# Four stages of a TensorE-bound kernel written in another order: FFT stages placed among matmul blocks, scaled grad_out kept on chip, w2 loaded early

## The chip, the cores and the metric

One core of a Trainium2 chip. The time is device microseconds (us) from start to end of one execution. A profile's *span* is the time from the first to the last instruction of one profiled execution, about 1.8 us below the time of that same execution.

## The reference

A gated sum of two branches and all its gradients:

```python
g = sigmoid((x * gate_w).sum(-1))             # x: [2048, 1024]
a = irfft2(rfft2(x) * (w_r + 1j * w_i))       # spectral branch
h = relu(B_x @ w1 + b1) ** 2                  # w1: [1024, 3584]
b = h @ w2 + b2                               # w2: [3584, 1024]
out = g * a + (1 - g) * b
# returned: out and the gradients of x, w_r, w_i, w1, b1, w2, b2, gate_w
```

The gradients of the dense branch flow only to its weights and, through the gate, to x. Work per stage, as the kernel cuts it:

- **rows, first FFT stage**: x and grad_out are transposed in blocks, the gate is computed, and each of 16 row tiles of x and of grad_out goes through the first transform (32 steps).
- **spectra**: 8 pairs of frequencies; forward transform, product with w, gradient of w, transform back (40 steps in the written program).
- **last FFT stage**: 32 steps, 16 for the output and 16 for the gradient of x.
- **h/dh**: 28 blocks of 128 hidden units, h and its gradient dh, with their transposes.
- **dW2, dW1**: 56 + 56 blocks of 16 matmuls.
- **out, input gradient**: 32 + 32 blocks of 28 matmuls.

## The kernel before

The kernel is written with a scheduler that orders each engine's instructions before the run. Tiles of one `tag` share `bufs` buffers. The parts that matter (cut):

```python
fps, fps_s = pool("fps", "right", PSUM)      # tag "ps2": 2 buffers of 2 banks, FFT stages
tps, tps_s = pool("tps", "right", PSUM)      # tag "tr": 2 buffers of 1 bank, transposes AND the spectra's small sp/si
...
# load_rows: for each of 16 row tiles
turned(xT, xt, i, nc.scalar.copy)            # 8 transposes, one copy
... gate of the row ...
db = fb.tile([P, D], BF16, name="db", tag="db", bufs=2)
nc.vector.tensor_scalar(out=db[:], in0=go[:], scalar1=omg[:, c_], ...)   # (1-g) * grad_out
turned(dbT, db, i, nc.vector.tensor_copy)    # only the transposed copy survives
one_s1(fb, cf, 0, i, xt, kf[:])              # first FFT stage of x
one_s1(fb, cf, 1, i, go, kg[:])              # ... and of grad_out
...
# mlp_grads: grad_out is loaded and scaled again, 16 times
ld(out=db[:], in_=go_perm[t])
nc.vector.tensor_scalar(out=db[:], in0=db[:], scalar1=omg[:, t : t + 1], ...)
...
# mlp_out: w2 (7 MB) is loaded at its start, w1T (7 MB) at its second block
for fc in range(0, FC, 4):
    ld(out=w2[:, fc : fc + 4, :], ...)
for k in range(S // BW):
    ...
    if k == 1:
        for fc in range(0, FC, 4):
            ld(out=w1T[:, fc : fc + 4, :], ...)
...
run(chain(load_rows(), fft_mid(), fft_out()))   # the order in which it is written
run(mlp_in())
run(mlp_grads())
...
run(mlp_out())
```

Of the kernel before, what the change touches and what calls it, by code (L numbers as in the profile page):

```python
# [10 lines left out]
P = 128  # L11
# [119 lines left out]
def kernel(  # L131
# [208 lines left out]
    def fft_mid():  # L340
# [3 lines left out]
        for m in range(S2 // 2):  # L344
# [5 lines left out]
            for T in range(2):  # L350
                z = fb.tile([P, 2, D], FDT, name="z", tag="z", bufs=3)
                ld(out=z[:], in_=z_scr[T][:].rearrange("c p l -> p c l")[:, m : m + 9 : 8, :])
                xs.append(spectrum(fb, T, m, z, am, sgn))
                yield 8
# [31 lines left out]
    def fft_out():  # L386
        fb, fbs = pool("f3", "right")
# [4 lines left out]
        for T in range(2):  # L392
            for i in range(NT):
# [20 lines left out]
                st(out=ax_scr[T][i][:], in_=yo[:])  # L414
                yield 2
        fbs.close()


    xT_p, xT_s = pool("xT")
# [3 lines left out]
    def load_rows():  # L423
        fb, fbs = pool("f1", "right")
        cf = fb.tile(list(consts["cf"].shape), FDT, name="cf", tag="cf")
        ld(out=cf[:], in_=cten["cf"].ap())
        b1row = fb.tile([FC, P], BF16, name="b1row", tag="b1row")
        ld(out=b1row[:], in_=B_b1.rearrange("(fc p) -> fc p", p=P))
        b1ps = tps.tile([P, FC], BF16, name="b1ps", tag="tr", bufs=2)
        nc.tensor.transpose(b1ps[:], b1row[:], identb[:FC, :FC])  # L430
        nc.vector.tensor_copy(out=b1col[:], in_=b1ps[:])
# [6 lines left out]

        for i in range(NT):
            xt = fb.tile([P, D], BF16, name="xt", tag="xt", bufs=3)  # L440
            ld(out=xt[:], in_=x_perm[i])
            turned(xT, xt, i, nc.scalar.copy)
            go = fb.tile([P, D], BF16, name="go", tag="go", bufs=3)
            ld(out=go[:], in_=go_perm[i])
            junk = fb.tile([P, D], BF16, name="junkt", tag="junkt")
            c_ = slice(i, i + 1)
            nc.vector.tensor_tensor_reduce(
                out=junk[:], in0=xt[:], in1=gatew_bc[:], scale=1.0, scalar=0.0,
                op0=ALU.mult, op1=ALU.add, accum_out=sgate[:, c_],
            )  # L450
            nc.scalar.activation(gcol[:, c_], sgate[:, c_], ACT.Sigmoid)
            nc.vector.tensor_scalar(out=omg[:, c_], in0=gcol[:, c_], scalar1=-1.0, scalar2=1.0, op0=ALU.mult, op1=ALU.add)
            db = fb.tile([P, D], BF16, name="db", tag="db", bufs=2)
            nc.vector.tensor_scalar(out=db[:], in0=go[:], scalar1=omg[:, c_], scalar2=None, op0=ALU.mult)
            turned(dbT, db, i, nc.vector.tensor_copy)
            kg = fb.tile([P, P], FDT, name="kg", tag="kg", bufs=2)
            nc.vector.tensor_scalar(out=kg[:], in0=kf[:], scalar1=gcol[:, c_], scalar2=None, op0=ALU.mult)
            one_s1(fb, cf, 0, i, xt, kf[:])
            one_s1(fb, cf, 1, i, go, kg[:])
            yield 8  # L460
        V(out=gpg[:], in0=gcol[:], in1=omg[:], op=ALU.mult)
# [77 lines left out]
    def column_sums(sb_pool, ps_pool, tag, acc, dst):  # L539

        row = sb_pool.tile([1, D], BF16, name="row", tag="row")
        for hf in range(NH):
            cs = slice(hf * H, (hf + 1) * H)
            pr = ps_pool.tile([1, H], FP32, name="prow", tag=tag, bufs=2)
# [5 lines left out]
    def mlp_grads():  # L550
        wb, wbs = pool("m2")
        mps, mpss = pool("mps2", "left", PSUM)
        res = []
        acc = wb.tile([P, D], FP32, name="dbacc", tag="dbacc")

        def group(scr, fg):
            t_ = wb.tile([P, NT, FGW], BF16, name="grp", tag="grp", bufs=2)
            ld(out=t_[:], in_=scr[fg][:])
            return t_

        nxt = None
        for t in range(NT):
            db = wb.tile([P, D], BF16, name=f"res0_{t}", tag=f"res0_{t}")
            ld(out=db[:], in_=go_perm[t])
            if t == 0:
                nxt = group(h2_scr, 0)
            nc.vector.tensor_scalar(out=db[:], in0=db[:], scalar1=omg[:, t : t + 1], scalar2=None, op0=ALU.mult)  # L567
            if t == 0:
                nc.vector.tensor_copy(out=acc[:], in_=db[:])
            else:  # L570
                V(out=acc[:], in0=acc[:], in1=db[:], op=ALU.add)
            res.append(db)
        jobs = [(h2_scr, fg) for fg in range(FG)] + [(dh_scr, fg) for fg in range(FG)]
        for n, (scr, fg) in enumerate(jobs):
# [10 lines left out]
            if scr is h2_scr:  # L585
                for fb_ in range(FGC):
                    wo = wb.tile([P, D], BF16, name="wo2", tag="wo2", bufs=2)
                    for hf in range(NH):
                        pw = mps.tile([P, H], FP32, name="pw", tag="pw", bufs=2)
                        for t in range(NT):  # L590
                            mm(  # L591
                                pw[:], lhsT=cur[:, t, fb_ * P : (fb_ + 1) * P], rhs=res[t][:, hf * H : (hf + 1) * H],
# [19 lines left out]
        wbs.close()  # L612

# [3 lines left out]
    def blocks(wb, scr):  # L617
        v_ = scr[:].rearrange("c p s -> p c s")

        def one(k):  # L620
            t_ = wb.tile([P, FC, BW], BF16, name="hblk", tag="hblk", bufs=2)
            ld(out=t_[:], in_=v_[:, :, k * BW : (k + 1) * BW])
            return t_
# [3 lines left out]
    def mlp_out():  # L627
        wp, wps = pool("w2p")
        w2 = wp.tile([P, FC, D], BF16, name="w2", tag="w2")
# [6 lines left out]
        for fc in range(0, FC, 4):  # L636
            ld(out=w2[:, fc : fc + 4, :], in_=B_w2[fc * P : (fc + 4) * P, :].rearrange("(q p) e -> p q e", p=P))
# [69 lines left out]
        column_sums(wb, mps, "acc2", gacc, out_8)  # L707
# [4 lines left out]
    def chain(*gens):  # L712
        for g_ in gens:
            yield from g_

    def run(gen):
        for _ in gen:
            pass

    run(chain(load_rows(), fft_mid(), fft_out()))  # L720
    run(mlp_in())
    run(mlp_grads())
    tps_s.close()
    fps_s.close()
    run(mlp_out())


# [28 lines left out]
```

## Time and profile before

| | kernel before |
|---|---|
| time, median of 3 | 1671.34 us (1670.29 to 1671.43) |
| span of the profiled run | 1667.4 us |
| mean granted TensorE clock | 0.948 |
| TensorE busy, VectorE busy | 1488.8 us (89%), 670.8 us (40%) |
| loads and stores | 267 MB, 160 GB/s |

TensorE is busy 89% of the span, but that counts slow matmuls and overlapping rows as full work. The slices and the stretches that the prediction prints are the better view: two regimes, one after the other, each with the other engine at rest.

### The profile page before, as it was taken

To read this page: it belongs to the slowest core of one execution; us is meant where nothing else is said; L and a number is where in the kernel's file an instruction comes from. 1 tells how busy PE (TensorE), PEld (TensorE's weight loads), DVE (VectorE), ACT (ScalarE), POOL (GpSimd) and SP (SyncE) were. 2 spreads that over 40 slices of the span, in tenths; PEclk is the share of its full clock that TensorE was granted. 3 is DMA by queue.
4 is the path that set the end of the run, shared out by engine and by line. 5 is a ranking of instruction groups with operands and counts; after the bars stand their busy time and mean duration, and the time that the engine had idled before them with its cause. 6 is when DMAs were issued, how large, how long until landed. Compare 5 with 4: busy or idle time off the path is not lost.

```text
span 1667.4 us, 20915 instructions
## 1 busy us (share of the span) xinstructions
PE 1488.8 (89%) x8482; PEld 732.5 (44%) x8482; DVE 670.8 (40%) x1334; ACT 437.2 (26%) x566; POOL 225.2 (14%) x395
## 2 busy tenths in 40 slices
PE   5655555799999999999959999999998999999997
PEld 4531111366555555555514444444443444444443
DVE  7846998666433333333361000000001555564232
ACT  6862222377533333333301111111110000000000
POOL 3330110122211111111110000111110000000000
PEclk9997676799999999999969999999999999999999
DMA  7536554468545655465488232323227853574340
GB/s 212 159 113 186 151 155 116 120 209 278 190 154 167 196 168 165 155 200 165 151 319 261 92 136 94 136 96 135 96 82 273 256 162 111 161 200 137 101 139 19
DMA packets 157194, 267.45 MB, mean 160 GB/s; under 512 B 10652, under 2 KB 90538, under 8 KB 155306
## 3 DMA queue, kind: packets, MB, share of 16 engines
q1 hardware_dynamic: 122890, 147.59, 28.6%
q0 software_dynamic: 34208, 118.53, 21.4%
q8 instruction: 66, 1.08, 0.3%
q14 instruction: 30, 0.25, 0.1%
HBM read 147.57 MB, written 118.51 MB: 160 GB/s over the span
## 4 chain that ended last, share of the span: by engine, by line
issue 68%; POOL 9%; PE 0%; ACT 0%; POOLq 0%; DVE 0%
POOL out_dram L609 2%; POOL dh_scr L524 1%; POOL out_dram L598 1%; POOL w1T_scr L510 1%; POOL h2T_scr L520 1%; POOL dhT_scr L521 1%; POOL ax_scr L414 1%; POOL out_dram L706 1%; POOL h_scr L523 1%; POOL out_dram L672 1%; PE pui L255 0%; ACT rt L401 0%; ACT e L405 0%; POOL out_dram L534 0%; POOLq L609 0%
## 5 line engine op out<-in xcount | busy, mean ns | idle before, releaser
L493 PE MATMUL ph<-xT,w1g 128*128 128x512 bf16 x896 | 226.8, 380 | 0.0
L591 PE MATMUL pw<-res,grp 128*128 128x512 bf16 x896 | 203.9, 388 | 18.0 <-DVE res L567 10.8
L499 PE MATMUL pd<-dbT,w2T 128*128 128x512 bf16 x896 | 215.3, 381 | 3.1 <-DVE w2T L486 3.1
L665 PE MATMUL acc<-w,hblk 128*128 128x512 bf16 x896 | 195.6, 382 | 6.1 <-DMA w<-in_B_w_dram 6.1
L666 DVE SCALAR_TENSOR_TENSOR ot<-acc,omg,af 128x512 bf16<-128x512 f32 x32 | 24.0, 750 | 437.7 <-PE acc L665 437.6
L603 PE MATMUL pw<-grp,res 128*128 128x512 bf16 x896 | 193.5, 379 | 0.0
L703 PE MATMUL accg<-w1Tr,hblk 128*128 128x512 bf16 x896 | 193.5, 379 | 0.0
L500 DVE SCALAR_TENSOR_TENSOR dhT<-pd,rT 128x512 bf16<-128x512 f32 x112 | 77.4, 691 | 258.2 <-PE pd L499 258.2
L591 PEld LDWEIGHTS <-grp 128*128 128x128 bf16 x896 | 88.7, 99 | 133.3 <-issue 26.4
L495 ACT ACTIVATE rT<-ph,b1col 128x512 bf16<-128x512 f32 x112 | 77.2, 689 | 238.6 <-PE ph L493 238.6
L665 PEld LDWEIGHTS <-hblk 128*128 128x128 bf16 x896 | 88.1, 98 | 113.6 <-DMA w<-in_B_w_dram 6.6
L499 PEld LDWEIGHTS <-w2T 128*128 128x128 bf16 x896 | 87.4, 98 | 106.5 <-DVE w2T L486 8.1
L703 PEld LDWEIGHTS <-hblk 128*128 128x128 bf16 x896 | 87.7, 98 | 105.7
L603 PEld LDWEIGHTS <-res 128*128 128x128 bf16 x896 | 87.7, 98 | 105.7
L493 PEld LDWEIGHTS <-w1g 128*128 128x128 bf16 x896 | 83.1, 98 | 72.7 <-issue 1.6
L595 ACT CAST wo<-pw 128x512 bf16<-128x512 f32 x56 | 32.7, 586 | 195.1 <-PE pw L591 195.1
L608 ACT CAST wo<-pw 128x512 bf16<-128x512 f32 x56 | 32.8, 586 | 160.6 <-PE pw L603 160.6
L255 PE MATMUL pu<-cf,ft 128*128 128x256 f16 (+3 forms) x256 | 38.7, 293 | 38.1 <-ACT ft L235 37.0
L496 ACT ACTIVATE h2T<-rT 128x512 bf16<-128x512 bf16 x112 | 70.6, 630 | 3.5
L704 DVE TENSOR_TENSOR gxo<-accg,g 128x512 bf16<-128x512 f32 x32 | 22.1, 691 | 105.1 <-PE accg L703 104.9
L319 PE MATMUL pv<-y,apmat 128*128 128x512 f16 x32 | 16.0, 549 | 53.9 <-DVE y L366 53.2
L609 POOL DMA_DIRECT2D out_dram<-wo x56 | 30.2, 540 | 163.2 <-ACT wo L608 158.7
(178 smaller groups left out, 1668.9 us busy)
## 6 DMA issues: line engine op xcount, KB each, us to landing
h2T_scr<-h2T POOLq DMA_DIRECT2D x28, 512.0 KB, 3.4
dhT_scr<-dhT POOLq DMA_DIRECT2D x28, 512.0 KB, 4.3
h_scr<-h2S POOLq DMA_DIRECT2D x14, 1024.0 KB, 8.0
dh_scr<-dhS POOLq DMA_DIRECT2D x14, 1024.0 KB, 10.6
grp<-h_scr SPq DMA_DIRECT2D x7, 2048.0 KB, 8.6
hblk<-h2T_scr SPq DMA_DIRECT2D x8, 1792.0 KB, 9.2
grp<-dh_scr SPq DMA_DIRECT2D x7, 2048.0 KB, 8.4
hblk<-dhT_scr SPq DMA_DIRECT2D x8, 1792.0 KB, 9.1
```

Of the source, the lines that this page charges most:

```text
L255: mm(pu[:, bank, lo : lo + n], lhsT=ft[:, b, :], rhs=mat[:, o : o + n], start=bool(f_ & 1), stop=bool(f_ & 2), skip_group_check=True,)
L493: mm(ph[:], lhsT=w1g[:, dc, fs], rhs=xT[:, dc, ss], start=(dc == 0), stop=(dc == DC - 1))
L495: nc.scalar.activation(rT[:], ph[:], ACT.Relu, bias=b1col[:, fc : fc + 1])
L496: nc.scalar.activation(h2T[:, ss], rT[:], ACT.Square)
L499: mm(pd[:], lhsT=w2T[:, ec, :], rhs=dbT[:, ec, ss], start=(ec == 0), stop=(ec == DC - 1))
L500: STT(out=dhT[:, ss], in0=pd[:], scalar=2.0, in1=rT[:], op0=ALU.mult, op1=ALU.mult, accum_out=gb1part[:, fc, sb : sb + 1],)
L591: mm(pw[:], lhsT=cur[:, t, fb_ * P : (fb_ + 1) * P], rhs=res[t][:, hf * H : (hf + 1) * H], start=(t == 0), stop=(t == NT - 1),)
L603: mm(pw[:], lhsT=xr[t][:, d_ * P : (d_ + 1) * P], rhs=cur[:, t, :], start=(t == 0), stop=(t == NT - 1),)
L608: nc.scalar.copy(out=wo[:], in_=pw[:])
L609: st(out=out_4[d_ * P : (d_ + 1) * P, fg * FGW : (fg + 1) * FGW], in_=wo[:])
L665: mm(acc[:], lhsT=cur[:, fc, t2 * P : (t2 + 1) * P], rhs=w2[:, fc, cs], start=(fc == 0), stop=(fc == FC - 1))
L703: mm(acc[:], lhsT=cur[:, fc, t2 * P : (t2 + 1) * P], rhs=w1T[:, fc, cs], start=(fc == 0), stop=(fc == FC - 1))
```

## The change

Its intent: put each piece of work that needs VectorE or ScalarE beside matmuls that don't. The core of the diff, cut:

```diff
+    dbn = db_p.tile([P, NT, D], BF16, name="dbn", tag="dbn")      # scaled grad_out, natural order, stays on chip
...
+        for i0 in range(0, NT, 4):          # four rows, then their x transforms, then one h/dh block
+            ...
+                nc.vector.tensor_scalar(out=dbn[:, i, :], in0=go[:], scalar1=omg[:, c_], ...)
+                turned(dbT, dbn[:, i, :], i, nc.vector.tensor_copy)
+            ...
+                one_s1(fb, cf, 0, i, xts[i - i0], kf[:])
+            yield
         for i in range(NT):                 # the grad_out transforms, later
             ...
+            one_s1(fb, cf, 1, i, go, kg[:])
+            yield
...
-            ld(out=db[:], in_=go_perm[t])   # mlp_grads: no second load and scaling
...
-                                pw[:], lhsT=cur[...], rhs=res[t][:, hf * H : (hf + 1) * H],
+                                pw[:], lhsT=cur[...], rhs=dbn[:, t, hf * H : (hf + 1) * H],
...
+                if T == 0 and i % 2 == 1:   # last FFT stage: w2 in pieces, long before out
+                    ...
+                        ld(out=w2[:, fc : fc + 4, :], ...)
...
-    run(chain(load_rows(), fft_mid(), fft_out()))
-    run(mlp_in())
-    run(mlp_grads())
+    for _ in rows:
+        for _ in range(1 if n < 4 else 6):  # h/dh units per row group, then per grad_out transform
+            next(units, None)
+    ...
+    for k, _ in enumerate(grads):           # spectra and half of the last stage among dW2/dW1
+        while done < todo * (k + 1) // per:
+            next(spec)
+            done += 1
+    for _ in outs:                          # the rest of the last stage among out
+        next(spec, None)
```

The spectra's z tile also goes from three buffers to two.

More of the change, by code (lines that the diff above doesn't have):

```diff
@@ L350, in fft_mid @@
             for T in range(2):
-                z = fb.tile([P, 2, D], FDT, name="z", tag="z", bufs=3)
+                z = fb.tile([P, 2, D], FDT, name="z", tag="z", bufs=2)
                 ld(out=z[:], in_=z_scr[T][:].rearrange("c p l -> p c l")[:, m : m + 9 : 8, :])
@@ L386, in fft_out @@
     def fft_out():
+        w2_p, w2_s = pool("w2p", "right")
+        w2 = w2_p.tile([P, FC, D], BF16, name="w2", tag="w2")
+        later["w2"], later["w2_s"] = w2, w2_s
         fb, fbs = pool("f3", "right")
@@ L414, in fft_out @@
                 st(out=ax_scr[T][i][:], in_=yo[:])
+                if T == 0 and i % 2 == 1:
+                    fc = 2 * (i - 1)
+                    if fc < FC:
+                        ld(out=w2[:, fc : fc + 4, :], in_=B_w2[fc * P : (fc + 4) * P, :].rearrange("(q p) e -> p q e", p=P))
                 yield 2
         fbs.close()
+    db_p, db_s = pool("db")
+    dbn = db_p.tile([P, NT, D], BF16, name="dbn", tag="dbn")
     xT_p, xT_s = pool("xT")
@@ L421, with rows_and_first_stage @@
     dbT = xT_p.tile([P, DC, S], BF16, name="dbT", tag="dbT")
-    def load_rows():
+    def rows_and_first_stage():
         fb, fbs = pool("f1", "right")
         cf = fb.tile(list(consts["cf"].shape), FDT, name="cf", tag="cf")
-        ld(out=cf[:], in_=cten["cf"].ap())
         b1row = fb.tile([FC, P], BF16, name="b1row", tag="b1row")
-        ld(out=b1row[:], in_=B_b1.rearrange("(fc p) -> fc p", p=P))
-        b1ps = tps.tile([P, FC], BF16, name="b1ps", tag="tr", bufs=2)
-        nc.tensor.transpose(b1ps[:], b1row[:], identb[:FC, :FC])
-        nc.vector.tensor_copy(out=b1col[:], in_=b1ps[:])
         def turned(dst, xt, i, eng):
@@ L437, in turned @@
             eng(out=dst[:, :, i * P : (i + 1) * P], in_=pt[:])
+        for i0 in range(0, NT, 4):
+            xts = []
+            for i in range(i0, i0 + 4):
+                xt = fb.tile([P, D], BF16, name="xt", tag="xt", bufs=4)
+                ld(out=xt[:], in_=x_perm[i])
+                xts.append(xt)
+            if i0 == 0:
+                ld(out=b1row[:], in_=B_b1.rearrange("(fc p) -> fc p", p=P))
+                b1ps = tps.tile([P, FC], BF16, name="b1ps", tag="tr", bufs=2)
+                nc.tensor.transpose(b1ps[:], b1row[:], identb[:FC, :FC])
+                nc.vector.tensor_copy(out=b1col[:], in_=b1ps[:])
+            for i in range(i0, i0 + 4):
+                xt = xts[i - i0]
+                c_ = slice(i, i + 1)
+                turned(xT, xt, i, nc.scalar.copy)
+                junk = fb.tile([P, D], BF16, name="junkt", tag="junkt")
+                nc.vector.tensor_tensor_reduce(
+                    out=junk[:], in0=xt[:], in1=gatew_bc[:], scale=1.0, scalar=0.0,
+                    op0=ALU.mult, op1=ALU.add, accum_out=sgate[:, c_],
+                )
+                nc.scalar.activation(gcol[:, c_], sgate[:, c_], ACT.Sigmoid)
+                nc.vector.tensor_scalar(out=omg[:, c_], in0=gcol[:, c_], scalar1=-1.0, scalar2=1.0, op0=ALU.mult, op1=ALU.add)
+                go = fb.tile([P, D], BF16, name="go", tag="go", bufs=3)
+                ld(out=go[:], in_=go_perm[i])
+                nc.vector.tensor_scalar(out=dbn[:, i, :], in0=go[:], scalar1=omg[:, c_], scalar2=None, op0=ALU.mult)
+                turned(dbT, dbn[:, i, :], i, nc.vector.tensor_copy)
+            if i0 == 0:
+                ld(out=cf[:], in_=cten["cf"].ap())
+            for i in range(i0, i0 + 4):
+                one_s1(fb, cf, 0, i, xts[i - i0], kf[:])
+            yield
@@ L439, in load_rows @@
+        V(out=gpg[:], in0=gcol[:], in1=omg[:], op=ALU.mult)
         for i in range(NT):
-            xt = fb.tile([P, D], BF16, name="xt", tag="xt", bufs=3)
-            ld(out=xt[:], in_=x_perm[i])
-            turned(xT, xt, i, nc.scalar.copy)
             go = fb.tile([P, D], BF16, name="go", tag="go", bufs=3)
             ld(out=go[:], in_=go_perm[i])
-            junk = fb.tile([P, D], BF16, name="junkt", tag="junkt")
-            c_ = slice(i, i + 1)
-            nc.vector.tensor_tensor_reduce(
-                out=junk[:], in0=xt[:], in1=gatew_bc[:], scale=1.0, scalar=0.0,
-                op0=ALU.mult, op1=ALU.add, accum_out=sgate[:, c_],
-            )
@@ L451, in load_rows @@
-            nc.scalar.activation(gcol[:, c_], sgate[:, c_], ACT.Sigmoid)
-            nc.vector.tensor_scalar(out=omg[:, c_], in0=gcol[:, c_], scalar1=-1.0, scalar2=1.0, op0=ALU.mult, op1=ALU.add)
-            db = fb.tile([P, D], BF16, name="db", tag="db", bufs=2)
-            nc.vector.tensor_scalar(out=db[:], in0=go[:], scalar1=omg[:, c_], scalar2=None, op0=ALU.mult)
-            turned(dbT, db, i, nc.vector.tensor_copy)
             kg = fb.tile([P, P], FDT, name="kg", tag="kg", bufs=2)
-            nc.vector.tensor_scalar(out=kg[:], in0=kf[:], scalar1=gcol[:, c_], scalar2=None, op0=ALU.mult)
@@ L458, in load_rows @@
-            one_s1(fb, cf, 0, i, xt, kf[:])
+            nc.vector.tensor_scalar(out=kg[:], in0=kf[:], scalar1=gcol[:, i : i + 1], scalar2=None, op0=ALU.mult)
             one_s1(fb, cf, 1, i, go, kg[:])
-            yield 8
-        V(out=gpg[:], in0=gcol[:], in1=omg[:], op=ALU.mult)
+            yield
         fbs.close()
@@ L537, in mlp_in, with column_sums @@
         xT_s.close()
-    def column_sums(sb_pool, ps_pool, tag, acc, dst):
+    def column_sums(sb_pool, ps_pool, tag, acc, dst, bufs=2):
         row = sb_pool.tile([1, D], BF16, name="row", tag="row")
@@ L543, in column_sums @@
             cs = slice(hf * H, (hf + 1) * H)
-            pr = ps_pool.tile([1, H], FP32, name="prow", tag=tag, bufs=2)
+            pr = ps_pool.tile([1, H], FP32, name="prow", tag=tag, bufs=bufs)
             mm(pr[:], lhsT=ones_f[:, 0:1], rhs=acc[:, cs], start=True, stop=True)
@@ L552, in mlp_grads @@
         mps, mpss = pool("mps2", "left", PSUM)
-        res = []
+        strm = later["strm"]
         acc = wb.tile([P, D], FP32, name="dbacc", tag="dbacc")
         def group(scr, fg):
-            t_ = wb.tile([P, NT, FGW], BF16, name="grp", tag="grp", bufs=2)
+            t_ = strm.tile([P, NT, FGW], BF16, name="grp", tag="strm", bufs=2)
             ld(out=t_[:], in_=scr[fg][:])
             return t_
-        nxt = None
-        for t in range(NT):
-            db = wb.tile([P, D], BF16, name=f"res0_{t}", tag=f"res0_{t}")
-            ld(out=db[:], in_=go_perm[t])
-            if t == 0:
-                nxt = group(h2_scr, 0)
-            nc.vector.tensor_scalar(out=db[:], in0=db[:], scalar1=omg[:, t : t + 1], scalar2=None, op0=ALU.mult)
-            if t == 0:
-                nc.vector.tensor_copy(out=acc[:], in_=db[:])
-            else:
-                V(out=acc[:], in0=acc[:], in1=db[:], op=ALU.add)
-            res.append(db)
         jobs = [(h2_scr, fg) for fg in range(FG)] + [(dh_scr, fg) for fg in range(FG)]
+        nxt = group(*jobs[0])
+        nc.vector.tensor_copy(out=acc[:], in_=dbn[:, 0, :])
+        for t in range(1, NT):
+            V(out=acc[:], in0=acc[:], in1=dbn[:, t, :], op=ALU.add)
         for n, (scr, fg) in enumerate(jobs):
@@ L591, in mlp_grads @@
                             mm(
-                                pw[:], lhsT=cur[:, t, fb_ * P : (fb_ + 1) * P], rhs=res[t][:, hf * H : (hf + 1) * H],
+                                pw[:], lhsT=cur[:, t, fb_ * P : (fb_ + 1) * P], rhs=dbn[:, t, hf * H : (hf + 1) * H],
                                 start=(t == 0), stop=(t == NT - 1),
@@ L612, in mlp_grads @@
         wbs.close()
+        db_s.close()
     BW = 2 * P
@@ L620, in one @@
         def one(k):
-            t_ = wb.tile([P, FC, BW], BF16, name="hblk", tag="hblk", bufs=2)
+            t_ = later["strm"].tile([P, FC, BW], BF16, name="hblk", tag="strm", bufs=2)
             ld(out=t_[:], in_=v_[:, :, k * BW : (k + 1) * BW])
@@ L627, in mlp_out @@
     def mlp_out():
-        wp, wps = pool("w2p")
-        w2 = wp.tile([P, FC, D], BF16, name="w2", tag="w2")
+        w2 = later["w2"]
+        wp, wps = pool("w1p")
         w1T = wp.tile([P, FC, D], BF16, name="w1Tr", tag="w1Tr")
@@ L635, in mlp_out @@
         nxt = load(0)
-        for fc in range(0, FC, 4):
-            ld(out=w2[:, fc : fc + 4, :], in_=B_w2[fc * P : (fc + 4) * P, :].rearrange("(q p) e -> p q e", p=P))
         for k in range(S // BW):
@@ L706, in mlp_out @@
                 st(out=o1_perm[t], in_=ot[:])
-        column_sums(wb, mps, "acc2", gacc, out_8)
+        column_sums(wb, mps, "acc", gacc, out_8, 4)
         mpss.close()
@@ L710, in mlp_out, with spectra @@
         wps.close()
-    def chain(*gens):
-        for g_ in gens:
-            yield from g_
-    def run(gen):
-        for _ in gen:
-            pass
-    run(chain(load_rows(), fft_mid(), fft_out()))
-    run(mlp_in())
-    run(mlp_grads())
-    tps_s.close()
+    later = {}
+    rows, units = rows_and_first_stage(), mlp_in()
+    n = 0
+    for _ in rows:
+        for _ in range(1 if n < 4 else 6):
+            next(units, None)
+        n += 1
+    strm_p, strm_s = pool("strm", "right")
+    later["strm"] = strm_p
+    for _ in units:
+        pass
+    def spectra():
+        yield from fft_mid()
+        yield from fft_out()
+    spec, grads = spectra(), mlp_grads()
+    todo = 5 * (S2 // 2) + NT
+    per = 2 * FG * FGC * NH
+    done = 0
+    for k, _ in enumerate(grads):
+        while done < todo * (k + 1) // per:
+            next(spec)
+            done += 1
+    tps_s.close()
+    outs = mlp_out()
+    for _ in outs:
+        next(spec, None)
+    for _ in spec:
+        pass
     fps_s.close()
-    run(mlp_out())
+    later["w2_s"].close()
+    strm_s.close()
 _INS = ['A_x', 'A_w_r', 'A_w_i', 'B_x', 'B_w1', 'B_b1', 'B_w2', 'B_b2', 'gate_w', 'grad_out']
```

## The prediction

> **What bounds the kernel now.** I read the page's slices first, then the costliest groups, then busy time by stretches that I cut at the stage borders, then the waits of TensorE, then timelines. The slices give the shape:
>
> ```profile
> PE   5655555799999999999959999999998999999997
> DVE  7846998666433333333361000000001555564232
> PEclk9997676799999999999969999999999999999999
> ```
>
> Each slice is 41.7 us. TensorE is at half in slices 0 to 7, full afterwards, with two dents: slice 20 (5, with the clock at 6) and slice 30. VectorE is near full in slices 2 to 7 and at 0 to 3 from slice 21 to 29. So the first 310 us are bound by other engines while TensorE idles, and the rest by TensorE while the others idle. Busy time by stretch (columns: stretch, its length, busy us of PE, PEld, DVE, ACT, POOL, the clock, the DMA share, GB/s):
>
> ```profile
> 8.70:125.00 116.30, 73.22 (x776) 56.91 (x776) 84.55 (x225) 87.31 (x98) 41.37 (x95) 1.00 0.50 159
> 125.00:310.00 185.00, 99.40 (x461) 35.12 (x461) 157.50 (x244) 45.44 (x39) 20.40 (x29) 0.69 0.52 143
> 310.00:445.00 135.00, 128.59 (x1004) 78.11 (x1004) 81.30 (x229) 88.25 (x102) 31.51 (x53) 0.95 0.67 217
> 445.00:843.00 398.00, 397.33 (x2650) 209.53 (x2647) 141.39 (x308) 149.43 (x214) 63.86 (x95) 1.00 0.53 168
> 843.00:878.00 35.00, 17.06 (x35) 4.41 (x36) 25.99 (x36) 1.07 (x2) 3.30 (x3) 0.53 1.02 388
> 878.00:1261.60 383.60, 382.25 (x1763) 172.28 (x1761) 5.30 (x7) 63.87 (x109) 45.35 (x84) 1.00 0.34 121
> 1261.60:1463.00 201.40, 195.34 (x896) 88.15 (x897) 100.78 (x200) 0.59 (x1) 8.63 (x16) 0.98 0.63 199
> ```
>
> The first row is the first FFT stage with the rows' transposes, the second the spectra (VectorE busy 157.5 of 185 us), the third the last FFT stage, already mixed with the h/dh blocks. So the order in which the program is written is not quite the order in which it runs: instructions of later stages were moved up where nothing held them. Then come h/dh alone, a gap, dW2 and dW1, and out; after 1463 us the same for the input gradient.
>
> ```profile
> PE pv L319 <- DVE y L366: 53.2, 16, 5.2
> PE pu L255 <- ACT ft L235: 37.0, 30, 1.9
> PE px L292 <- DVE pm L281: 22.5, 8, 3.0
> PE pw L591 <- DVE res L567: 10.8, 15, 1.6
> PE acc L665 <- DMA w<-in_B_w_dram: 6.1, 1, 6.1
> ```
>
> These are TensorE's waits (us in all, times, longest): on the spectra's VectorE products, on ScalarE's copy between the two matmuls of the first stage, on grad_out being scaled a second time, and on w2 being loaded at the start of out. Each is a thing that the change goes at.
>
> **What the Trainium skill says.** Four places bear on this.
> - "TensorE: Matmul & The Clock Gate", section "What's actually happening": the array runs at half clock by default and reaches full clock only after a sustained busy window. The trace agrees: clock 0.69 in the spectra and 0.53 in the gap at 843 us, 1.00 elsewhere. So gaps cost twice, once as idle time and once as slow matmuls after them.
> - The same page, "Step-by-step: what each phase is for": weight loads may be pulled ahead, but matmuls stay in program order. A spectrum matmul placed too early among the dW2 blocks therefore holds up the blocks behind it. The trace before can't show that for the spectra; for the last FFT stage it shows how little it can cost (below).
> - "Perfetto Trace Analysis", "Optimization Strategy": where the most-contended engine changes over time, interleave the regimes. This is the change.
> - The same page, "Identifying the Most-Contended Engine": matmul busy time is a poor measure as matmuls are pipelined. Here a 512-column matmul has a row of 379 ns, but in the last stretch 896 of them take 193.3 us, 0.2158 us each. I count work by spacing, not by the rows' durations.
>
> **TensorE's own work at full clock**, by start-to-start spacing in stretches without waits:
> - Four groups of 896 matmuls of 512 columns (dW2, dW1, out, input gradient): 896 x 0.2158 = 193.3 us each, 773.2 in all.
> - h/dh: from one transposition of w2 (456.45 us) to the next (473.24) is 16.8 us, with 64 matmuls and 48 transposes. 28 of them: 470.4.
> - One step of the first or last FFT stage: 8 matmuls of 128 columns 0.45 us, then 8 of the column stage 1.01 us, so 1.46; 32 + 32 of them: 93.4. The pattern is here, amid h/dh:
>
> ```profile
> 341.12 0.50 PE L516 MATMUL ptr<-identb,dhT 128*128 128x128 bf16 x6
> 341.49 0.61 PE L484 MATMUL ptw<-identb,w2r 128*128 128x128 bf16 x8
> 341.94 0.81 PE L493 MATMUL ph<-xT,w1g 128*128 128x512 bf16 x3
> 342.86 1.17 PE L255 MATMUL pui<-ci,rt 128*128 128x512 f16 x8
> 343.87 0.61 PE L399 MATMUL pki<-ki,r 128*128 128x128 f16 x8
> 344.31 1.24 PE L493 MATMUL ph<-xT,w1g 128*128 128x512 bf16 x5
> ```
>
> Blocks are split around FFT steps without a gap, and in 310 to 445 us TensorE waited just 0.5 us for ScalarE's rt.
> - Rows' transposes: 32 times 8, 0.45 us each: 14.4.
> - Spectra: a forward step is 8 long matmuls and 8 tiny ones (8 x 0.2158 + 8 x 0.026 = 1.94), a backward step measures 1.88 at full clock (140.33 to 142.16 us and the like). 16 of each: 61.1.
>
> Sum 1412.5. With 8.7 us before the first transpose, 1.9 for the column sum of grad_out and 10.9 from the last matmul of the input gradient to the end (1656.5 to 1667.4), the floor of this order of work is 1434.0 us. The kernel before has 1667.4 - 1434.0 = 233 us above it. I place them so: 8.7 to 125: 116.3 - 62.8 (14.4 + 46.7 and eight early h matmuls, 1.7) = 53.5. Spectra to 310: 185 - about 57 (61.1 less the last two backward steps) = 128. 310 to 843: 533 - (470.4 - 1.7 + 46.7 + 3.8) = 14. dW2 and dW1 with the gap (843 to 1261.6): 418.6 - 386.6 - 1.9 = 30. Out: 201.4 - 193.3 = 8. That sums to 233.5.
>
> **The change part by part.**
> - First phase. For each row only the x transform stays with the row work; the 16 grad_out transforms go among h/dh. VectorE per row: gate reduction 1.3, four adds of one transform's fold at 0.34 from start to start = 1.36, omg 0.1, scaling 0.48, transposed copy 0.69: 3.9; h/dh for the first block adds 6.5 us over 16 rows, 0.4. 4.3 x 16 = 69 us. ScalarE: xT 1.03, gate 0.2, ft 1.01, u 1.31 = 3.55, with h 3.95 a row, 63 us. TensorE: 2.36 a row plus 16.8 = 54.6 us. VectorE binds; before, it was busy 89% of 8.7 to 40 us in such a stretch, so 69 / 0.92 = 75 us. Phase end near 84 us; loss 75 - 54.6 = 20 instead of 53.5. Gain 33.
> - h/dh with the grad_out transforms: 27 x 16.8 + 16 x 1.46 = 477 us, TensorE-bound, as VectorE needs 6.5 and ScalarE 6.3 of each 16.8 us. Loss 8 instead of 14 (the cold restart of slice 7 is gone). Gain 6.
> - dW2 from scaled grad_out kept on chip: no 16 loads of 256 KB, no 16 scalings, no wait on them; the clock stays up. The 19 us of summing on VectorE stay, off the path. One spectrum step after every two dW blocks (6.9 us): 40 steps over 80 blocks. VectorE's 157.5 us of spectra spread over 80 x 3.45 + 61 = 337 us, half busy, so the spectra become TensorE's 61.1 us, plus what waits they bring. Then 16 last-stage steps over the other 32 blocks. I give 3 us to the transition and 12 to waits in this stretch: about 0.2 us for each of 56 steps, more than the 0.5 us for 32 steps seen before, as VectorE's chain (two products of 1.23, two sums of 0.69, 3.8 us) and loads from memory are longer. Gain 128 + 30 - 15 = 143.
> - Out: w2 comes in seven 1 MB loads during dW, so the 6.1 us wait and its cold restart go. The last 16 steps run one per block; VectorE then has (0.75 + 0.68 + half of 4.5) + 1.7 = 5.4 us per 7.5 us, the tightest place, but with four acc buffers. Loss 4 instead of 8. Gain 4.
> - z with two buffers instead of three: one load less ahead; with 13 us between steps of TensorE time against 5.6 us to landing, free.
>
> Sum of gains: 33 + 6 + 143 + 4 = 186, and the last-stage steps that move cost the same everywhere. I take 5 us back for things not seen: span 1667.4 - 181 = 1486; the timed median is 3.9 us above the span: 1490 us.
>
> **Rivals.**
> - The spectra stall the in-order TensorE. For: the long chain z, pm, px, x, products, y, pv, pc, with matmuls twice in it whose place among the blocks is fixed before the run; single buffers for x, v, t, pm; loads in one queue, where the load queue's own waits before reach 46 us. Each step that stalls over 3 us would also drop the clock. At 1 us more for each of 40 steps: 1530 us. Against: 0.5 us lost in 32 steps of the last stage, and two dW blocks of slack around each step.
> - The first phase doesn't shrink: if ScalarE and VectorE alternate in waiting for each other as they do now (ScalarE 87 and VectorE 85 of 116 us), it takes 95 us: 1510.
> - The first phase hides better: if later h/dh blocks are moved up into its idle TensorE time, up to 20 us more go: 1470. Against: before, only eight matmuls of h/dh were moved up into 300 us; the transposed tiles share two PSUM buffers with the row work.
> - DMA becomes the bound in dW: before it is 0.34 there; spectra traffic at 0.52 of 185 us adds 0.52 x 185 / 460 = 0.21, w2 some more. Under 0.65 on average: not a bound, so no change.
>
> **Range and chances.** From floor plus 20 us of loss (1434 + 20 + 4 = 1458) to the stall rival (1530) gives 8 in 10. Nearly all outcomes are below 1638, 2% less than before; only a serious misplacement could miss it. Predicted 1490 us, range 1460 to 1532; faster 0.97, same 0.02, slower 0.01.
>
> **What would show it right or wrong.** Right: the slices have 9 for PE from slice 2 to 38 with a clock of 1.0 throughout; VectorE at 3 to 6 in the dW slices; no wait of pw on res and none of acc on w2; the phase before the second h/dh chunk ends near 84 us; dW stretch near 490 us. Wrong: a clock under 0.9 in the dW slices, waits of pv on y or px on pm above 15 us in total, or h/dh filling that starts only after 95 us. A dW stretch above 520 us would mean the stall rival.

## The result

1484.72 us (median of 4, 1483.41 to 1485.25) against 1671.38 us; ratio 0.8881, 95% interval 0.8865 to 0.8896. A ratio is the mean time of one kernel's fast runs over that of the other's fast runs of the same rounds, so not quite the ratio of the medians quoted. The span is 1482.7 us and the mean clock 0.994.

The slices of the changed kernel (one digit per 37 us):

```profile
PE   6899999999999997999999999999989999999998
DVE  7953343343433335555554443211455655562222
PEclk9999999999999999999999999999999999999999
```

TensorE is full from the third slice on, with a dent in the 16th slice (from 556 us) and one in the 30th (from 1075 us); VectorE never stays full after the second slice; the clock shows no dent. The stages as stretches (columns: stretch, length, busy us of PE, PEld, DVE, ACT, POOL, clock, DMA share, GB/s):

```profile
9.20:82.20 73.00, 61.48 (x617) 45.34 (x623) 66.91 (x170) 55.39 (x70) 24.48 (x54) 1.00 0.67 216
82.20:565.40 483.20, 474.82 (x3231) 258.62 (x3285) 181.75 (x417) 205.49 (x276) 86.92 (x152) 1.00 0.56 181
565.40:1052.50 487.10, 473.85 (x2464) 223.66 (x2513) 213.94 (x354) 140.97 (x181) 79.95 (x135) 0.99 0.57 192
1052.50:1280.70 228.20, 221.91 (x1145) 107.95 (x1165) 130.85 (x289) 34.90 (x35) 17.83 (x33) 0.99 0.61 193
```

In order: rows with the x transforms, h/dh with the grad_out transforms, dW with the spectra and half of the last stage, out with the other half. The input gradient takes the rest, as before. (Some matmul records are missing from this trace, 149 of 8482, so its busy time for PE is a little low.) The spectra, which took 185 us with VectorE busy 157.5, have no stretch of their own any more: VectorE is busy 213.94 of 487.1 us beside dW.

TensorE's waits (us in all, times, longest):

```profile
PE b1ps L453 <- DMA b1row<-in_B_b_dram: 9.2, 1, 9.2
PE px L292 <- DMA z<-z_scr: 8.4, 1, 8.4
PE pu L255 <- ACT ft L235: 5.8, 12, 1.4
PE pki L402 <- DMA r<-y_scr: 3.8, 1, 3.8
```

The first is the start of the program. Of the waits on VectorE that the prediction lists, none is left; ft fell from 37.0 to 5.8 us. Two single waits on loads stand out, and they are the two dents. The first, on TensorE's timeline (start, length, operation, count, idle time before):

```profile
567.88 14.42 PE L604 MATMUL pw<-dbn,grp 128*128 128x512 bf16 x65
590.67 0.59 PE L292 MATMUL px<-z,amat 128*128 128x512 f16 x1 [8.38 <-DMA z<-z_scr]
591.05 0.63 PE L293 MATMUL px<-z,amat 128*128 128x512 f16 x1
...
594.51 0.38 PE L292 MATMUL px<-z,amat 128*128 128x512 f16 x1
```

TensorE has nothing it may do before the first spectrum's z, and after the gap the same matmul has a row of 0.59 to 0.63 us instead of 0.38 until 594.3: the granted clock was 0.50 from 590.6 to 594.3 us. dW2's later blocks were not short of operands; they stood behind px in program order.

### The profile page after: what moved, and what is told of

Read it like the earlier page. It is cut to its first block, busy times and chain, and to the rows that moved or that the text cites. A ratio compares the mean times of both kernels' runs of the same rounds, so it can differ in the third digit from the quotient of the medians.

```text
span 1482.7 us, 20756 instructions
## 1 busy us (share of the span) xinstructions
PE 1426.7 (96%) x8333; PEld 723.4 (49%) x8482; DVE 669.2 (45%) x1319; ACT 438.2 (30%) x564; POOL 219.9 (15%) x395
## 5 line engine op out<-in xcount | busy, mean ns | idle before, releaser
L520 PE MATMUL pd<-dbT,w2T 128*128 128x512 bf16 x883 | 211.5, 379 | 1.7 <-DVE dhT L521 1.0
L514 PE MATMUL ph<-xT,w1g 128*128 128x512 bf16 x850 | 211.6, 379 | 1.4
L616 PE MATMUL pw<-grp,res 128*128 128x512 bf16 x870 | 198.2, 379 | 1.3
L604 PE MATMUL pw<-dbn,grp 128*128 128x512 bf16 x872 | 195.5, 379 | 1.2
L715 PEld LDWEIGHTS <-hblk 128*128 128x128 bf16 x896 | 87.7, 98 | 105.7
L410 DVE TENSOR_TENSOR tt<-e 128x512 f16<-128x512 f16 x32 | 13.6, 425 | 139.8 <-ACT e L408 139.3
L306 DVE CAST x<-px 128x1024 f16<-128x1024 f32 x16 | 19.6, 1225 | 120.7 <-PE px L305 120.6
L404 ACT CAST rt<-pki 128x1024 f16<-128x1024 f32 x32 | 32.5, 1015 | 78.0 <-PE pki L402 78.0
```

The source lines that it names most:

```text
L404: nc.scalar.copy(out=rt[:], in_=pk[:])
L514: mm(ph[:], lhsT=w1g[:, dc, fs], rhs=xT[:, dc, ss], start=(dc == 0), stop=(dc == DC - 1))
L520: mm(pd[:], lhsT=w2T[:, ec, :], rhs=dbT[:, ec, ss], start=(ec == 0), stop=(ec == DC - 1))
L604: mm(pw[:], lhsT=cur[:, t, fb_ * P : (fb_ + 1) * P], rhs=dbn[:, t, hf * H : (hf + 1) * H], start=(t == 0), stop=(t == NT - 1),)
L616: mm(pw[:], lhsT=xr[t][:, d_ * P : (d_ + 1) * P], rhs=cur[:, t, :], start=(t == 0), stop=(t == NT - 1),)
L715: mm(acc[:], lhsT=cur[:, fc, t2 * P : (t2 + 1) * P], rhs=w1T[:, fc, cs], start=(fc == 0), stop=(fc == FC - 1))
```

## The experiments

Twelve kernels ran, on three chips, beside runs of the kernel before on the same chip (medians there 1672.27, 1669.62 and 1666.83 us). All gave correct results. Costs in us below are differences of medians from the changed kernel's 1484.72. It was run at another time. The medians of the kernel before differ by up to 5.4 us, so where a cost is only a few us, the waits in the trace count for more than the difference. The diffs are cut to the lines that matter.

**1. The written order of the spectra** (e1_spectra_first)

```diff
     spec, grads = spectra(), mlp_grads()
+    for _ in spec:
+        pass
     for k, _ in enumerate(grads):
-        while done < todo * (k + 1) // per: next(spec); done += 1
```

> All 40 spectrum steps and all 32 last-stage steps are written ahead of dW2 instead of among dW2, dW1 and out; the rest is the changed kernel. Theory A (the written order is what hides the spectra): TensorE again idles while VectorE makes the spectra, about 120 us more than the changed kernel (185 us alone against 61 us of TensorE work), so near 1600 us with a clock near 0.7 in that stretch. Theory B (what held later work back was the shared PSUM buffers of the transposes, and dW2 needs none of them, so its matmuls are moved up into the gaps anyway): within 25 us of the changed kernel, 1480 to 1510 us, clock above 0.97. I lean to B.

1497.5 us, ratio 0.8951: 12.8 us more. Theory B, not A. Two stretches of it, in the columns of the stretches above:

```profile
650.00:700.00 50.00, 49.89 (x289) 22.47 (x288) 49.90 (x80) 18.17 (x20) 9.69 (x15) 1.00 0.75 234
700.00:750.00 50.00, 49.45 (x284) 22.38 (x282) 49.56 (x80) 20.14 (x22) 10.09 (x15) 1.00 0.67 206
```

VectorE runs the spectra without a pause and TensorE is full too: dW2's blocks, written behind all spectra, were moved up between them. So the fine interleaving in the source isn't what hides the spectra here. Most of the 12.8 us are lost before these stretches: from 600 to 650 us TensorE is busy 40.26 us at clock 0.90, and its waits of pv on VectorE's y come to 7.9 us.

**2. The first stage** (e2_s1_with_rows)

```diff
                 one_s1(fb, cf, 0, i, xts[i - i0], kf[:])
+                one_s1(fb, cf, 1, i, gos[i - i0], kg[:])   # again with the rows
-        for i in range(NT): ... one_s1(fb, cf, 1, i, go, kg[:]); yield
```

> The grad_out transforms of the first stage go back to the rows; the rest is the changed kernel. My term for this part was 33 us of the gain: the first phase would end near 125 us again instead of 82, with 23.4 us less TensorE work left after it, and the loss of 20 us there grows to about 50. So 1484.7 + 30 = about 1515 us. Rival: h/dh blocks are now written right behind each group of rows and fill more of the phase, then under 10 us, below 1495.

1491.51 us, ratio 0.8917: 6.8 us more, not 30. The rival was right. Its stretch after the 82.2 us at which the changed kernel's first phase ends:

```profile
82.20:125.00 42.80, 36.78 (x339) 24.76 (x340) 25.57 (x69) 34.27 (x37) 15.90 (x38) 1.00 0.34 124
```

The transforms do run on to about 125 us, but TensorE is busy 36.78 of those 42.8 us, as h/dh blocks run there too. The last h/dh transposes start at 570.9 us instead of 565.1. (The edit also gives the grad_out tiles four buffers instead of three.)

**3. The kept grad_out** (e3_reload)

```diff
-                rhs=dbn[:, t, hf * H : (hf + 1) * H]
+                rhs=res[t][:, hf * H : (hf + 1) * H]      # loaded and scaled again in mlp_grads, as before
```

> dW2 takes grad_out loaded and scaled a second time, as before, instead of the copy kept on chip; the rest is the changed kernel. If the gap at 843 us of the kernel before (35 us with 7.6 us worth of matmuls in it) comes back, about 25 us more: 1510 us, with waits of pw on res. Rival: the first spectrum steps now fill that gap, or its loads come early because the queue is free: under 8 us more, as spectrum and dW2 both wait for the same load queue either way.

1496.12 us, ratio 0.8945: 11.4 us more, between the two expectations. The waits of dW on what it needs:

```profile
PE pw L612 <- DVE res L589: 7.0, 10, 1.2
PE px L292 <- DMA z<-z_scr: 4.2, 1, 4.2
```

The wait on res is there, as in the kernel before (10.8 us), while the wait on z shrinks. z comes at the same time (first px at 590.18 us, 590.67 in the changed kernel), but dW2's first matmuls now run later and fill more of the time before it.

**4. The early w2** (e4_w2_late)

```diff
-        w2_p, w2_s = pool("w2p", "right")                 # in fft_out, loaded there in pieces
+        w2 = wp.tile([P, FC, D], BF16, name="w2", tag="w2")   # in mlp_out, loaded at its start
```

> w2 is loaded at the start of out, into the space that x leaves after dW1, as before; the rest is the changed kernel. My term: about 8 us at the start of out come back (6.1 us wait and a cold restart), so near 1492 us, with a wait of acc on the load of w2. Rival: the last FFT stage's steps fill the wait, so 0 to 3 us; a second rival: the 7 MB of w2 then meet the 7 MB of w1 and the last stage's loads in the same 80 us, so 15 us or more.

1489.25 us, ratio 0.8903: 4.5 us more, between the theory and its first rival. The intervals of the two ratios (0.8889 to 0.8916 here, 0.8865 to 0.8896 for the change) overlap, so the size isn't clear of noise; the waits are what shows a cost. TensorE's waits in its out stage, 8.2 us where the changed kernel has 3.8:

```profile
PE pui L255 <- ACT rt L401: 4.4, 3, 1.6
PE acc L672 <- DMA w<-in_B_w_dram: 2.7, 1, 2.7
PE pki L399 <- DMA r<-y_scr: 1.1, 1, 1.1
```

The first acc matmul starts at 1064.3 us, 12 us after dW1's last; the last FFT stage's steps fill most of that, as the first rival said, but run unmixed and wait for ScalarE.

**5. What ties the parts together** (e9_before_reordered). The four parts undone one at a time cost 12.8 + 6.8 + 11.4 + 4.5 = 35.5 us; the change gained 187. So the parts can't be added, and I tried the kernel before with nothing but its stages reordered:

```diff
-    run(chain(load_rows(), fft_mid(), fft_out()))
-    run(mlp_in())
+    run(load_rows())
+    run(mlp_in())
+    run(chain(fft_mid(), fft_out()))
     run(mlp_grads())
```

> The kernel before with nothing changed but the order in which its parts are written: rows with first FFT stage, h/dh, then spectra and last FFT stage, then dW2/dW1 and out (spectra and last stage behind h/dh instead of ahead of it). Theory (partners): what the change gains is mostly that the spectra, which need VectorE, now lie beside dW2/dW1, which leave VectorE free, instead of before and beside h/dh, which needs VectorE 6.5 us in each 16.8 us; the fine interleaving, grad_out kept on chip and w2 early only add the 7 to 13 us each that undoing them cost (7 + 13 + 11 + 4.5 = 36). Then this is near 1485 + 36 = 1521 us, 1505 to 1545. Rival (the parts depend on each other): without the interleaved order and the kept grad_out, dW2 can't start beside the spectra as its own loads and scalings queue behind theirs on VectorE: above 1580 us.

1625.68 us, ratio 0.9747. My theory fell, by 100 us; the rival was right. Two stretches amid its spectra, and the scalings of grad_out for dW2 (the two times: first and last start):

```profile
650.00:700.00 50.00, 27.03 (x126) 10.15 (x126) 47.88 (x78) 13.55 (x11) 6.42 (x9) 0.69 0.71 213
700.00:750.00 50.00, 29.95 (x132) 10.75 (x132) 48.25 (x75) 12.94 (x11) 7.09 (x10) 0.67 0.38 118
```

```profile
L567 DVE TENSOR_SCALAR res<-res,omg x16: 474/478/533, 622.3 to 779.0; 128x1024 bf16<-128x1024 bf16 x16
```

dW2 is next to the spectra in program order, yet TensorE is half idle at clock 0.67 to 0.69, because each dW2 block needs all sixteen scaled tiles, and those sixteen scalings of 0.48 us stand on VectorE behind spectrum work until 779 us. Late loads don't explain it: the sixteen loads of grad_out were all issued by 625.4 us, and a load of res took at most 11.6 us to land. Compare experiment 1: there VectorE is as full, but dW2's operands lie ready on chip, so TensorE is full too. And experiment 3: there grad_out is rescaled, but the spectra come in doses, so the scalings get through. Laid out (us):

| | spectra in doses | spectra all ahead of dW2 |
|---|---|---|
| grad_out kept on chip | 1484.7 (the change) | 1497.5 (experiment 1) |
| grad_out scaled again | 1496.1 (experiment 3) | 1625.7 (this one) |

The last cell also lacks the early w2, the moved first-stage transforms and the h/dh blocks written between the row groups, so its 141 us above the change aren't all due to the two parts. The traces tell them apart. The last h/dh transposes start at 585.5 us there and at 565.1 in the changed kernel, so 20 us were lost before the spectra. From the end of h/dh to the end of dW1 (1218.3 us) it takes 632 us for 496 us of work (dW, spectra and the whole last stage, by the prediction's count), a loss of 136 us; the changed kernel loses 14 in its dW stretch. Either of the two parts keeps VectorE from standing between TensorE and dW2; with neither, about 120 us of the gain are gone.

**6. What kept h/dh out of the spectra's gaps before** (e8_before_tr_free, on the kernel before)

```diff
-        sp = tps.tile([P, 2, 2, 2], FP32, name="sp", tag="tr", bufs=2)     # and "si" likewise
+        sp = fps.tile([P, 2, 2, 2], FP32, name="sp", tag="ps2", bufs=2)
```

> The kernel before with one thing changed: the spectra's two small PSUM tiles share the buffers of the other FFT tiles instead of those of the transposes. Theory: in the kernel before h/dh could not be moved up among the spectra because its transposes take the two shared PSUM buffers in written order, behind the spectra's; freed from that, h/dh fills the spectra's gaps and 60 to 120 us go: 1550 to 1610 us. Rival: what keeps h/dh out is the written order itself or space: within 20 us of 1671, or slower, as the spectra now have one PSUM buffer less.

1637.11 us, ratio 0.9804 (0.9774 to 0.9833): 32.5 us less than the kernel before, so the shared buffers did hold h/dh back, but far less came of it than expected. Its spectra stretch, and in the same stretch the VectorE instructions that finish dh (product and accumulator read, two rows each):

```profile
135.00:330.00 195.00, 133.63 (x711) 59.52 (x718) 169.92 (x276) 58.70 (x59) 26.27 (x37) 0.75 0.56 167
```

```profile
135.00:330.00 195.00, 6.23 (x18) 0.75 0.56 167
```

Nine dh pieces, of 112: 2.25 of 28 h/dh blocks ran among the spectra, and five more pieces before 135 us, beside the rows. The balance: by the end of the spectra 60 us of h/dh work are done (233 matmuls of 512 columns at 0.2158 us, 176 transposes at 0.055 us), against 1.7 us before, but the spectra end 21.3 us later (last pv at 329.8 instead of 308.5 us). The 37 us that are left fit the 34 us by which dW2 starts earlier (816.2 instead of 850.1 us). VectorE is busy 169.92 of 195 us, so I read it as the new limit: an h/dh block needs 6.5 us of VectorE by the prediction's count. That h/dh is the wrong partner for the spectra and dW the right one is what this and experiment 1 show together; that VectorE alone set the 2.25 is argued, not isolated.

**7. The stall at z.** First guess: the load queue (e5_x_late).

```diff
             if n == 1:
                 column_sums(wb, mps, "pw", acc, out_7)
+            if n == FG - 2:
                 xr = []          # the 16 loads of x for dW1, written four groups later
```

> The 16 loads of x for dW1 are written at the sixth dW2 group instead of the second; the rest is the changed kernel. Theory: the one large stall left in dW2 (8.4 us for the first z, with a cold restart after it) is made by the load queue: its x loads wait 46 us at the head for the h/dh space to come free and 4 MB then go ahead of the first spectrum's loads. Then the wait of px on z falls below 2 us and the time by 8 to 11 us, to about 1475 us. Rival: z itself waits for space or for its own data (z_scr was last written at 492 us, so unlikely): no change, 1484.

1483.89 us, ratio 0.8894, and the edit did nothing: the loads were moved up again. This is the queue's timeline at the place, in that kernel:

```profile
562.01 15.15 SPq L597 DMA_DIRECT2D res<-in_A_x_dram  x15
...
582.78 0.98 SPq L352 DMA_DIRECT2D z<-z_scr  x2
```

So it decides nothing about the queue. But loads written later going ahead means that z's loads could not go earlier, which points at z's space. In the changed kernel the spectra's w and z loads are issued at 582.05 and 583.49 us. h/dh's last dh store, issued at 567.57 us, took 14.3 us to land by the list of issues, so until 581.9 us, and the queue's own waits name that store as what w waited for:

```profile
SPq L348 <- DMA dh_scr<-dhS: 2.6, 1, 2.6
```

Second guess, then: the spectra's tiles lie in space that h/dh's staging tiles occupy. The test gives z and amat a space of their own (e10_z_space), with a control for the buffer that had to be given up for it (e12_w1t_single):

```diff
+        fa, fas = pool("f2a", "right")
         fb, fbs = pool("f2", "right")
-            am = pair_mats(fb, "amat", m)
+            am = pair_mats(fa, "amat", m)
-                z = fb.tile([P, 2, D], FDT, name="z", tag="z", bufs=2)
+                z = fa.tile([P, 2, D], FDT, name="z", tag="z", bufs=2)
-                        w1T = wb.tile([P, DC, P], BF16, name="w1T", tag="w1T", bufs=2)   # control: this alone
+                        w1T = wb.tile([P, DC, P], BF16, name="w1T", tag="w1T", bufs=1)
```

> The changed kernel with the spectra's z and amat tiles in a space of their own that doesn't overlap h/dh's working tiles (and one buffer instead of two for h/dh's w1T, to make the room). x late changed nothing, as its loads were moved up again. Theory now: the first z waited 8 us since its space was h/dh's staging space, which comes free only when the last dh store has landed. With its own space z is loaded before h/dh ends: the 8.4 us wait and the cold matmuls behind it go, 7 to 11 us, about 1475 us. Rival: the spectra then wait for the weights w, still in shared space, so the stall moves on to pv: within 3 us of 1484.7.

> Control for the two kernels before: only the single buffer for w1T in h/dh, nothing else. Expected within 2 us of 1484.7; if it is slower, that much is to be added to what the space is worth.

Control 1484.53 us (ratio 0.8900): the buffer is free. With the space, 1480.16 us (0.8874): 4.4 us less than the control, about half of what I expected. TensorE's timeline, and one of VectorE's waits from 560 to 600 us:

```profile
564.55 0.38 PE L292 MATMUL px<-z,amat 128*128 128x512 f16 x1
...
595.33 1.01 PE L319 MATMUL pv<-y,apmat 128*128 128x512 f16 x2 [3.73 <-DVE y L367]
```

```profile
DVE x L306 <- DMA dh_scr<-dhS: 6.0, 1, 6.0
```

The space was the cause: z's loads are now issued from 499.71 us on, the first px starts at 564.55, before h/dh has ended, and the wait on z is gone. The rival was right that a stall would move on to pv, 3.73 us of it, but the trace shows no wait of VectorE on w. What it shows is the same store again: VectorE's copy into x, whose tile is still in the shared space, waited 6.0 us for it, until 581.63 us. Then seven additions for the column sum of grad_out, 1.22 us each, ran on VectorE among the products, and the first y came only at 594.50 us. Which of the two the stall is due to wasn't tested.

**8. The stall at r** (e6_w1_spread). In the changed kernel, the load queue and TensorE around the second dent:

```profile
1061.04 14.48 SPq L656 DMA_DIRECT2D w1Tr<-w1T_scr  x7
1083.45 0.36 SPq L636 DMA_DIRECT2D hblk<-h2T_scr  x1
1083.92 7.29 SPq L661 DMA_DIRECT2D a__10426<-ax_scr  x1
...
1091.74 0.90 SPq L398 DMA_DIRECT2D r<-y_scr  x2
```

```profile
1097.57 1.04 PE L402 MATMUL pki<-ki,r 128*128 128x128 f16 x8 [3.81 <-DMA r<-y_scr]
1098.40 2.34 PE L677 MATMUL acc<-w,hblk 128*128 128x512 bf16 x5
1100.53 2.13 PE L255 MATMUL pui<-ci,rt 128*128 128x512 f16 x8
```

```diff
-            if k == 1:
-                for fc in range(0, FC, 4):
+            if k >= 1:
+                for fc in range(4 * (k - 1), 4 * k, 4):
                     ld(out=w1T[:, fc : fc + 4, :], ...)    # one of seven pieces per block
```

> The seven 1 MB loads of w1 in out are spread over blocks 1 to 7 instead of all at block 1; the rest is the changed kernel. Theory: the stall of 3.8 us on r at 1097 us and the cold matmuls after it come from 7 MB of w1 and a block of h queued in front of r: the wait goes and 6 to 8 us are won, about 1478 us. Rival: r waits because the queue's head waits for a buffer (acc or yo), whatever w1 does: within 2 us of 1484.7.

1478.17 us, ratio 0.8857: 6.5 us less, and 5.7 less than experiment 7's first guess, whose edit did nothing. The wait on r is gone from TensorE's list, and the out stage:

```profile
1052.00:1273.90 221.90, 219.35 (x1142) 106.74 (x1162) 130.34 (x289) 34.72 (x35) 17.90 (x33) 1.00 0.62 198
```

221.9 us instead of 228.2. The rival had a part of it. In the changed kernel no r is issued between 1060.67 and 1091.74 us: first w1's seven loads take the queue until 1075.5, then hblk stands at its head, 7.8 us for a free buffer, and the load of the last stage's output (a__10426) waits 5.1 us for VectorE to make it (yo). With w1 spread such waits are still there (5.6 and 6.2 us), and the next pair of r is issued at 1091.49 us, no earlier; but two more r went out before it, at 1067.74 and 1075.48 us, between the pieces of w1.

**Both fixes**: x late with w1 spread (e7_both)

> Both of the two edits before, x late and w1 spread. If the two stalls are separate the gains add: 1468 to 1472 us, TensorE's waits on loads below 2 us after the start.

gave 1478.67 us, ratio 0.8858, the same as w1 spread alone, as x late was no fix. The space for z with w1 spread (e11_z_space_w1)

> The edit before together with w1's loads spread over seven blocks. If the two gains add: 1484.7 - 6.5 - 9 = about 1469 us, clock 0.998 or more, and TensorE's waits on loads near 0 after the first 10 us.

gave 1476.17 us, ratio 0.8849: 8.4 us below the control of the same call, the fastest version here. Alone the two gave 4.4 and 6.5, so 8.4 of 10.9 us are there together. The 1469 us expected had counted 9 us for z; the stall that moved to pv (4.0 us in this kernel) is part of what is missing, the rest stays open.

## Why the prediction was right, and where it was not

- **The floor by spacing** (1434 us) and the claim that the rest is idle or slow TensorE time held: the span came out at 1482.7 us, 48.7 us above it.
- **The signs named**: no wait of pw on res and none of acc on w2 is left, waits of pv on y or px on pm are gone, and the clock has no dent. Two signs were missed: PE has a 7 and an 8 in the slices of the two stalls, and VectorE falls to 1 and 2 in three dW slices (from 927 us), where 3 to 6 was said, as its spectra are done by then.
- **First phase**: the time was right (end at 82.2 us; 84 predicted), and so was the count behind it (VectorE busy 66.9 of 73.0 us; 69 of 75 predicted). What was wrong is where the gain comes from. The prediction put all 33 us down to moving the grad_out transforms out of the phase. Experiment 2 puts that at 6.8 us, as h/dh fills TensorE while the transforms run. In experiment 5's kernel, with h/dh behind all rows, h/dh ends 14.6 us later than in experiment 2's, with rows in groups and h/dh between them (585.5 and 570.9 us). So the grouping seems to be worth more than the move, but no run took it away alone. The predicted 1490 us didn't need that attribution, only the phase's end.
- **h/dh with the grad_out transforms**: 485 us predicted, 483.2 measured.
- **dW with the spectra**: the work is 386.6 + 61.1 + 1.9 + 23.4 = 473.0 us; with 3 us for the transition and 12 for waits that makes 488 ("near 490"), and 487.1 were measured. That it is so close is luck, as two errors cancel. Of the 14.1 us lost the transition took about 10.2, not 3: 8.4 us were one wait for the first z, and 3.6 us of half-speed matmuls behind it cost about 1.8 us. The 12 us were meant as 0.2 us for each of 56 steps; what is left, 3.9 us, is 0.07 us a step. The stall rival, 1 us for each step, didn't come.
- **The split of the gain.** "Gain 128 + 30 - 15 = 143" treats hiding the spectra and dropping the second scaling as separate terms. They aren't: either alone gets nearly all of it, and the loss without both is about 120 us (experiment 5).
- **Out**: a loss of 4 us predicted, 228.2 - 216.7 = 11.5 us measured. This is the term that was mis-sized. It looked for trouble on VectorE ("the tightest place"); it was the load queue, where w1's 7 MB and the two waits behind it stood before the last stage's r. Experiment 8 takes 6.5 us of it away. Also, w2 early was worth about 4.5 us, close to the gain of 4 that the stage as a whole was given.
- **"5 us back for things not seen"** roughly covered that: the tail after the last input-gradient matmul was 2 to 3 us shorter than before (8.4 against 10.9 us; up to the issue of the last store both take 2.9 us, and what follows I didn't look into), and the timed median is 2.0 us above the span where 3.9 were assumed. The 3.9 set the span of one execution against the median of others; that execution itself took 1669.16 us, 1.8 above its span.
- **The rivals**: "only eight matmuls of h/dh were moved up" had its cause where the prediction put it, in the two shared PSUM buffers, but experiment 6 shows that freeing them gives 32.5 us and not the spectra's whole loss. DMA as a bound: the share beside dW is 0.57, under the 0.65 said, so no bound on average; but both stalls that are left come out of stretches where it was full (1.03 from 568 to 582 us, 1.07 from 1061 to 1092 us).
- **Small misreadings**, without effect on the sum: VectorE is near full only in slices 4 to 6 of the kernel before (9, 9, 8), not in 2 to 7; and the clock outside the spectra and the gap is not 1.00 throughout, two of the printed rows have 0.95 and 0.98. That z needs only two buffers wasn't tested alone; after the first z, TensorE's list has no wait on z.

## What to carry to other kernels

Choose the partner of a stage by the engine that it leaves free, and then check that the partner's operands don't pass through the busy engine: next to a full VectorE, dW2 ran at full rate with its operand ready on chip and at half rate when sixteen scalings of 0.48 us stood in VectorE's queue. Don't add up what each part of a change is worth from undoing it alone; where two parts remove the same obstacle, each looks cheap, and only a run without both shows the size. Once TensorE is full, look for single waits on loads and ask what the load really waits for, space or the queue: here one stall came from shared space and one from a burst in the queue, and a few lines won back 4.4 us of one and 6.5 us of the other.

## What the Trainium skill lacked or had wrong

- "TensorE: Matmul & The Clock Gate", section "Back-to-back issue gap": it gives about 131 ns for 512 columns and 81 ns for 128 as the sustained spacing of weight load and matmul pairs. The runs here show 215.8 ns (896 matmuls of the input gradient in 193.3 us, each with its own weight load) and 55 ns (8 transposes in 0.44 to 0.45 us), which is what that section calls the isolated gap. The measurement decides: with its sustained figure the floor would have been far too low.
- "Perfetto Trace Analysis", section "Identifying the Most-Contended Engine": weight-load busy share as a measure of distance to the roofline. It is 45% (87.7 of 193.3 us) in the input-gradient stage, where TensorE has no gap at full clock, and 49% of the changed kernel's span. With 98 ns of weight load per 215.8 ns matmul it can't come near 100%, so the share says little without that ratio.
- No page has it: work placed among other work shares more than engines. A tile's space that overlaps another stage's staging tiles makes a load wait until that stage's last store has landed (14.3 us after issue here), and TensorE 8.4 us with it.
